# A first block normalized in two halves straight from PSUM, and a filter stage whose evacuations may run on either engine

## The chip, the cores and the metric

One core of a Trainium2 chip. The metric is the device time of one execution in microseconds, median of several; the profile's span is some 2 us shorter (129.6 us for a run of 131.36 us). PE is TensorE, DVE is VectorE, ACT is ScalarE, POOL is GpSimd. "Wait" means that an engine's next instruction is held by a semaphore. An execution counts as slow when it is over 1.5% above the fastest of its kernel; the others are the fast runs.

## The reference, cut to what matters

```python
x = A_x                                                       # (1, 2048, 512), bf16
h = x + irfft2(rfft2(layernorm(x)) * (w_r + 1j * w_i))         # the filter
h2 = h + mlp(layernorm(h))    # mlp: layernorm again, w1 over the sequence, gelu, w2 over the sequence
```

The kernel does the transforms as matmuls. The sequence is cut into 16 blocks n2 of 128 rows. After the filter each block must be transformed back (Bi, evacuation Bie, Ai), added to x, normalized (HH), and only then is it an operand of the first MLP product, which sums over the blocks (`m1_t_n2`, tile t of the hidden size). So the first block's way from the filter to HH is a serial chain.

## The kernel before

All instructions are placed by a builder: each has a name and one or several engines it may run on, and named lists fix the order per engine. The semaphores follow from the dependencies.

```python
    # filter stage: B (transform over d), evacuation Be, C (16 x 16 transform), evacuation Ce, product P with w, I, evacuation Ie
    NB = 4                                       # buffers of Bsb and of P
    K.op(f"Be{c}", "act", ...activation(Bb[c % NB], ps[:, b, :], ACT.Copy)...)         # ScalarE only
    K.op(f"Ce{tag}", "act", ...activation(dst, src, ACT.Copy)...)                      # ScalarE only
    ...
    # after the filter, blocks n2 = 0, 1, 2 ("early"): the identity matmul ID adds x inside PSUM
    def emit_h(n2):      # early blocks: copy PSUM to H
        K.op(f"h{n2}", "dve", ...tensor_copy(H[:, n2, :], ps[:, bA, :])...)
    def emit_sq(n2):     # sum of squares about the mean, ScalarE, from PSUM for early blocks
        K.op(f"sq{n2}", "act", ...activation(sq, hsrc, ACT.Square, bias=nm[:, n2, 0:1], accum_out=s2t[:, n2, 0:1])...)
    def emit_A2(n2):     # reciprocal root
        K.op(f"A2_{n2}", "act", ...activation(A2[:, n2, 0:1], s2t[:, n2, 0:1], ACT.Abs_reciprocal_sqrt, ...)...)
    def emit_hh(n2):     # normalize, from the copy in H
        K.op(f"hh{n2}", "dve", ...tensor_scalar(HH[:, n2, :], H[:, n2, :], nm[:, n2, 0:1], A2[:, n2, 0:1], op0=ALU.add, op1=ALU.mult)...)
    # later blocks: sd (sum and difference of the two parities) on VectorE, one Ai matmul, h = PSUM + x, sq, A2, hh
    ...
    "dve": "... P14 P15 Ie14_0 Ie15_0 Bie1 Bie2 h0 hh0 h1 sd3_1 sd3_0 hh1 h2"
```

In these lists a name is a group of instructions and its number the block or group: B, C, I, Bi, Ai are groups of matmuls on PE; a trailing e (Be, Ce, Ie, Bie) is the evacuation of such a group, its copy from PSUM to SBUF; P is a product with the filter weights on VectorE; m1 is the first MLP product; sd, sq, A2, h and hh are the steps of the normalization. HH is the normalized block that m1 reads.

## Time and profile before

| | before |
|---|---|
| time, median (range) | 131.52 us (131.19 to 131.54, 3 runs) |
| span of the profiled run | 129.6 us |
| busy: PE, DVE, ACT | 94%, 49%, 50% |
| filter, first to last matmul | 19.90 us |
| last filter matmul to first MLP matmul | 5.18 us |
| first MLP matmul to last matmul of all | 84.24 us |

The last three rows come from the starts of single matmuls in the trace. They are the measure used below, because the start of the filter itself moves between executions: in the 14 traces of this study it lay between 16.46 and 17.21 us, which is as large as most effects here. The sum of the three rows is 109.32 us. A start-to-start distance is the only fair look at PE: a shown matmul overlaps the next one (a 512-wide one is shown as 0.379 us and issued every 0.216), so PE looks busy where it idles by less than about 0.16 us. Some traces lack a few matmuls (nine in the one of before, none in the one of after, against the weight loads); a missing 512-wide one leaves a hole of exactly one issue time (0.216 us) and is not counted as idle.

### The profile page before, as it was taken

To read this page: it belongs to the slowest core of one execution; us is meant where nothing else is said; L and a number is where in the kernel's file an instruction comes from. 1 tells how busy PE (TensorE), PEld (TensorE's weight loads), DVE (VectorE), ACT (ScalarE), POOL (GpSimd) and SP (SyncE) were. 2 spreads that over 40 slices of the span, in tenths; PEclk is the share of its full clock that TensorE was granted. 3 is DMA by queue.
4 is the path that set the end of the run, shared out by engine and by line. 5 is a ranking of instruction groups with operands and counts; after the bars stand their busy time and mean duration, and the time that the engine had idled before them with its cause. 6 is when DMAs were issued, how large, how long until landed. Compare 5 with 4: busy or idle time off the path is not lost.

```text
span 129.6 us, 2028 instructions
## 1 busy us (share of the span) xinstructions
PE 122.1 (94%) x772; PEld 73.5 (57%) x781; DVE 63.5 (49%) x135; ACT 64.3 (50%) x137; POOL 11.8 (9%) x33
## 2 busy tenths in 40 slices
PE   6969989999998999999999999999999999999990
PEld 2346667777764455555444444456666666666660
DVE  1699917999948767668664000000422423323322
ACT  4699879989968487787787932222000000000000
POOL 0068980200000000000000000000000000000000
DMA  3999888999999999999000000000112112121121
GB/s 83 369 395 366 239 216 182 281 337 378 403 419 411 427 416 420 273 331 374 33 0 0 0 0 0 5 0 0 40 40 81 40 55 69 42 77 44 40 81 43
DMA packets 16505, 22.71 MB, mean 175 GB/s; under 512 B 1552, under 2 KB 12304, under 8 KB 16368
## 3 DMA queue, kind: packets, MB, share of 16 engines
q1 hardware_dynamic: 15808, 21.66, 48.2%
q10 hardware_dynamic: 576, 0.92, 1.9%
q0 software_dynamic: 112, 0.01, 0.3%
q8 instruction: 6, 0.10, 0.3%
q14 instruction: 3, 0.02, 0.0%
HBM read 20.49 MB, written 2.10 MB: 174 GB/s over the span
## 4 chain that ended last, share of the span: by engine, by line
PE 82%; DMA 5%; ACT 3%; SPq 3%; DVE 2%; issue 1%; POOL 0%; DVEq 0%; ACTq 0%
PE ps L839 29%; PE ps L919 27%; DMA F<-c_F 5%; PE ps L769 5%; PE ps L690 5%; PE ps L637 5%; PE ps L651 3%; SPq L490 3%; PE ps L806 2%; PE ps L593 2%; PE ps L925 2%; ACT Xsb L664 2%; ACT Y L607 1%; ACT Bsb L641 1%; DVE OUT L931 1%
## 5 line engine op out<-in xcount | busy, mean ns | idle before, releaser
L839 PE MATMUL ps<-HH,W 128*128 128x512 bf16 (+1 forms) x172 | 41.4, 379 | 0.7 <-DVE HH L831 0.6
L919 PE MATMUL ps<-GT,W 128*128 128x512 bf16 (+1 forms) x162 | 35.7, 379 | 0.2
L931 DVE SCALAR_TENSOR_TENSOR OUT<-ps,B2f,H 128x512 bf16<-128x512 f32 x16 | 12.0, 752 | 44.8 <-PE ps L919 24.4
L919 PEld LDWEIGHTS ps<-GT,W 128*128 128x128 bf16 (+1 forms) x165 | 23.8, 144 | 11.9
L839 PEld LDWEIGHTS ps<-HH,W 128*128 128x128 bf16 (+1 forms) x176 | 16.8, 100 | 18.4 <-issue 1.3
L901 ACT ACTIVATE GT<-ps,B1f 128x512 bf16<-128x512 f32 (+1 forms) x11 | 7.0, 692 | 10.8 <-PE ps L839 10.8
L815 DVE TENSOR_TENSOR H<-ps,X 128x512 bf16<-128x512 f32 x13 | 9.0, 691 | 6.8 <-PE ps L806 6.8
L672 DVE TENSOR_TENSOR P<-Xsb,W 128x1024 bf16<-128x1024 bf16 x16 | 10.5, 686 | 3.6 <-ACT Xsb L664 3.6
L821 ACT ACTIVATE SQ<-H,nm 128x512 bf16<-128x512 bf16 x13 | 9.4, 721 | 4.7 <-DVE H L815 4.7
L559 DVE BATCH_NORM_STATS2 st<-X 128x6 f32<-128x512 bf16 x13 | 8.2, 677 | 3.2 <-DMA X<-in_A_x_dram 3.2
L769 PE MATMUL ps<-GD,TT 128*128 128x256 bf16 x64 | 9.6, 273 | 0.1
L779 ACT ACTIVATE EO<-ps 128x512 bf16<-128x512 f32 x14 | 8.1, 581 | 2.6 <-PE ps L769 2.6
L690 PE MATMUL ps<-Hm,P 128*128 128x128 bf16 x128 | 9.3, 220 | 0.1
L641 ACT ACTIVATE Bsb<-ps 128x512 bf16<-128x512 f32 x16 | 8.8, 613 | 0.7 <-PE ps L637 0.7
L593 PE MATMUL ps<-FS,X 128*128 128x256 bf16 x64 | 7.8, 272 | 1.3 <-POOL FS L577 1.3
L637 PE MATMUL ps<-E,Y 128*128 128x256 bf16 x64 | 8.3, 273 | 0.7 <-ACT Y L607 0.7
L664 ACT ACTIVATE Xsb<-ps 128x1024 bf16<-128x1024 f32 (+1 forms) x10 | 8.6, 873 | 0.7 <-PE ps L651 0.4
L690 PEld LDWEIGHTS ps<-Hm,P 128*128 128x128 bf16 x128 | 7.5, 98 | 2.0 <-issue 1.3
L769 PEld LDWEIGHTS ps<-GD,TT 128*128 128x128 bf16 x64 | 6.1, 97 | 3.9 <-ACT TT L706 0.4
L577 POOL TENSOR_SCALAR FS<-F,rs 128x256 bf16<-128x256 bf16 x16 | 7.4, 482 | 7.6 <-ACT rs L565 7.2
L533 PE MATMUL ps<-WM 128*128 128x512 bf16 (+1 forms) x19 | 6.6, 500 | 1.2 <-DVE eps L525 1.2
L593 PEld LDWEIGHTS ps<-FS,X 128*128 128x128 bf16 x64 | 5.5, 97 | 3.7 <-POOL FS L577 2.3
(51 smaller groups left out, 92.7 us busy)
## 6 DMA issues: line engine op xcount, KB each, us to landing
W<-in_B_w_dram SPq DMA_DIRECT2D x8, 688.0 KB, 12.2
W<-in_B_w_dram SPq DMA_DIRECT2D x10, 512.0 KB, 18.0
out_dram<-OUT SPq DMA_DIRECT2D x16, 128.0 KB, 1.7
X<-in_A_x_dram SPq DMA_DIRECT2D x4, 256.0 KB, 6.1
F<-c_F SPq DMA_DIRECT2D x4, 256.0 KB, 6.4
IF<-c_IF SPq DMA_DIRECT2D x1, 1024.0 KB, 7.8
W<-in_A_w_r_dram SPq DMA_DIRECT2D x4, 224.0 KB, 3.6
W<-in_A_w_i_dram SPq DMA_DIRECT2D x4, 224.0 KB, 3.7
```

The lines of the kernel that those rows point to most:

```text
L593: r = eng.matmul(ps[:, b, 256 * u:256 * u + 256].rearrange("p (a b) -> p a b", a=2), X[:, n2, 128 * t:128 * t + 128], fr if t < 2 else fa, ...
L637: r = eng.matmul(o, Y[:, k, c, :], E[:, k, :].rearrange("p (h r) -> p h r", h=2), start=(i == 0), stop=(i == 3), skip_group_check=True)
L641: K.op(f"Be{c}", "act", lambda e, eng: eng.activation(Bb[c % NB][:, :], ps[:, b, :], ACT.Copy), ins=[ps[:, b, :]], outs=[Bb[c % NB][:, :]] ...
L664: K.op(f"Ce{tag}", "act", lambda e, eng: eng.activation(dst, src, ACT.Copy), ins=[ps[:, b, :] for b in banks], outs=[Xb[i][:, :, cs[0] % 2 ...
L672: return eng.tensor_tensor(P[:, :, :, :], x.unsqueeze(2).broadcast_to([NP, 2, 2, 256]), W[:, 2 * c:2 * c + 2, :, :], ALU.mult)
L690: r = eng.matmul(o, P[:, h, m, par::2], Hm[:, v, m, :].rearrange("p (m r) -> p m r", r=4), start=(h == 0 and m == 0 and (par == 0 or b != ...
L769: r = eng.matmul(o, TT[:, q, n2, par, :], GD[:, par, q, :], start=(i == 0), stop=(i == 3), skip_group_check=True)
L815: K.op(f"h{n2}", "dve", lambda e, eng: eng.tensor_tensor(H[:, n2, :], ps[:, bA, :], X[:, n2, :], ALU.add), ins=[ps[:, bA, :], X[:, n2, :]] ...
L821: K.op(f"sq{n2}", "act", lambda e, eng: eng.activation(sq[:, :], hsrc, ACT.Square, bias=nm[:, n2, 0:1], accum_out=s2t[:, n2, 0:1]), ins=[h ...
L839: return eng.matmul(ps[0:Mt, bank, :], W1[:, n2, 128 * t:128 * t + Mt], HH[:, n2, :], start=(n2 == 0), stop=(n2 == 15), skip_group_check=True)
L919: r = eng.matmul(ps[:, b, :], W2[t][0:Kt, n2::16], GT[0:Kt, t, :], start=(t == 0), stop=(t == NFT - 1), skip_group_check=True)
L931: K.op(f"fin{n2}", "dve", lambda e, eng, n2=n2, b=b: eng.scalar_tensor_tensor(OUT[:, n2, :], ps[:, b, :], B2f[:, n2:n2 + 1], H[:, n2, :], ...
```

## The change

The intent: (a) take the first block past the filter in two halves of d, in banks of their own, with statistics by `bn_stats` on VectorE and the normalization straight from PSUM, the copy to H later; (b) a newly searched order for the first twelve blocks; blocks 1 and 2 also normalized from PSUM; (c) in the filter, B and C evacuations on either engine, six buffers of Bsb and P, and a new order. Its core:

```diff
-    NB = 4
+    NB = 6
-        K.op(f"Be{c}", "act", ... activation ...)
+        K.op(f"Be{c}", ("act", "dve"), ... activation if e == "act" else tensor_copy ...)
-        K.op(f"Ce{tag}", "act", ... activation ...)
+        K.op(f"Ce{tag}", ("act", "dve"), ... activation if e == "act" else tensor_copy ...)
 # PSUM banks of the early blocks moved: bank_E 1:3 2:4 3:2, else 7; bank_A 1:5 2:0, else 6
     def emit_hh(n2):
+        src = ps[:, bank_A(n2), :] if n2 < NEARLY else H[:, n2, :]
-        ... tensor_scalar(HH[:, n2, :], H[:, n2, :], nm, A2 ...)
+        ... tensor_scalar(HH[:, n2, :], src, nm, A2 ...)
+    def emit_first():                      # block 0; m = 0, 1: left half in bank 6, right half in bank 7
+        ID0m, Bi0m (two matmuls each), Bie0m (256 wide, either engine), Ai0em, Ai0om
+        bq0m: bn_stats(sc[:, 6*m:6*m+6], ps[:, bk, 0:256])      # VectorE
+        aq0:  bn_aggr(sc[:, 16:18], sc[:, 0:12])
+        A2_0: activation(A2[:, 0, 0:1], sc[:, 17:18], Abs_reciprocal_sqrt, ...)
+        hh0m: tensor_scalar(HH[:, 0, half m], ps[:, bk, 0:256], nm, A2)
+        h0m:  copy of the half to H, prio 63                     # after the normalization
+    for t in range(NACC): for m in range(2): m1_t_0{l,r}         # first MLP matmuls of block 0 in halves
 # per-engine lists, filter part:
-  pe  "B0 B1 B2 B3 C0 C1 B5 B4 C2p I0 B7 B6 I1 C4p I3 B8 B9 C6p I2 B10 B11 I4 C8p I5 ... I9 B15 I8 C14 I10 C15 I11 I12 I13 I14 I15"
+  pe  "B0 B1 B2 C0 B3 C1 B5 B4 C2p I0 B6 B7 C4p B8 B9 I1 C6p I2 B10 I3 B11 C8p ... B15 I7 I8 I9 C14 C15 I10 I11 I12 I13 I14 I15"
-  dve "... P0 P1 Ie0 P3 P2 Ie1 Ie3 P4 P5 ... Bie1 Bie2 h0 hh0 h1 sd3_1 sd3_0 hh1 h2"
+  dve "... Be2 P0 Be5 P1 Ie0 Be6 P2 P3 Be8 P5 P4 ... P15 Ie13 Ie15_0 Bie00 bq01 bq00 aq0 hh01 hh00 h01 h00 sd3_1 sd3_0 hh1 h3 sd4_1 sd4_0 h1 hh2 ..."
```

## The prediction

> **What bounds the kernel now.** I read the page first: busy shares, then the chain that ended last.
>
> ```profile
> span 129.6 us, 2028 instructions
> PE 122.1 (94%) x772; PEld 73.5 (57%) x781; DVE 63.5 (49%) x135; ACT 64.3 (50%) x137; POOL 11.8 (9%) x33
> PE 82%; DMA 5%; ACT 3%; SPq 3%; DVE 2%; issue 1%; POOL 0%; DVEq 0%; ACTq 0%
> ```
>
> PE (TensorE) carries 82% of the chain; no other engine exceeds 5%. But a shown matmul overlaps its neighbours, so a busy share hides small gaps. I therefore cut the span where the stages meet, and compare each stretch with the issue time of its matmuls (columns: stretch, its length, then each engine's busy time and count).
>
> ```profile
> 16.79:36.96 20.17, 19.98 (x257) 15.56 (x259) 16.25 (x26) 18.44 (x32) 3.21 (x8) 1.00 0.99 312
> 36.96:41.87 4.91, 4.30 (x30) 2.54 (x29) 2.97 (x7) 3.33 (x10) 0.00 (x0) 1.00 1.01 414
> 41.87:68.06 26.19, 26.03 (x141) 13.04 (x145) 18.75 (x53) 20.13 (x52) 0.00 (x0) 1.00 0.77 285
> 68.06:88.47 20.41, 20.31 (x95) 9.63 (x95) 1.42 (x3) 8.74 (x15) 0.00 (x0) 1.00 0.00 1
> 88.47:126.53 38.06, 37.86 (x172) 25.06 (x174) 11.28 (x16) 0.67 (x1) 0.00 (x0) 1.00 0.15 52
> ```
>
> These are the filter (16.79 to 36.96), the way from the filter to the first MLP matmul, the inverse transform interleaved with the first MLP product, the rest of that product, and the second product. The last holds 176 matmuls: 38.06/176 = 0.216 us each, full rate. The third holds about 84 MLP matmuls and 13 inverse ones of 512 columns (97 x 0.216 = 20.95) and 12 blocks of four 256-column ones (0.435 each in the chain, 5.2): 26.15 of 26.19, no gap. So from 41.87 on the end is fixed by PE work; only what PE idles before can be won, and what it would idle newly is lost.
>
> In the filter, chain pieces give 0.87 for two B groups, 0.45 for an I group after a B and 0.55 after a C, 0.54 for a pair of Cs, 0.33 for a single C. 16 B (6.96), 7 C pairs (3.78), 2 singles (0.66), 16 I (7.12) and some 9 changes after a C at 0.1 (0.9) are 19.4 of 20.17: about 0.75 us idle. Between 36.96 and 41.87 PE has two warm-up matmuls, three identity, three A groups of two 512-equivalents and four B groups: 5 x 0.216 + 3 x 0.43 + 4 x 0.435 = 4.1 of 4.91, so 0.8 idle. That idle time is mostly one wait:
>
> ```profile
> 40.99 0.27 PE L802 MATMUL ps<-EO,IF 128*128 128x256 bf16 x1
> 41.87 1.24 PE L839 MATMUL ps<-HH,W 128*128 128x512 bf16 x5 [0.61 <-DVE HH L831]
> ...
> 39.91 0.69 DVE L780 CAST EO<-ps 128x512 bf16<-128x512 f32 x1 [0.40 <-PE ps L769]
> 40.51 0.68 DVE L812 CAST H<-ps 128x512 bf16<-128x512 f32 x1
> 41.31 0.41 DVE L831 TENSOR_SCALAR HH<-H,nm,A 128x512 bf16<-128x512 bf16 x1
> ```
>
> VectorE evacuates block 2, copies block 0 to H and normalizes from the copy; only then has PE its first MLP operand.
>
> **What the Trainium skill says.** "TensorE: Matmul & The Clock Gate", Back-to-back issue gap, gives 518 cycles for 512 columns and 262 for 256, or 216 and 109 ns at 2.4 GHz. The trace agrees (0.216; 0.435 for four of 256), so halving a matmul costs almost no streaming. "Perfetto Trace Analysis", Optimizing Scalar/DVE Operations, says that breaking up instructions may let work complete sooner where ScalarE or VectorE makes bubbles, at a fixed cost per access: a 512-wide VectorE copy from PSUM takes 0.692 us here, a 256-wide one 0.415, not half. "VectorE: DVE Perf Modes", Why PSUM operands drop a tier, holds that an fp32 PSUM operand runs at the slow rate: normalizing from bf16 SBUF takes 0.41 here, a 512-wide PSUM read 0.69. So two halves from PSUM will take about 0.77 together against 0.41, in exchange for not waiting for the copy.
>
> **The change, part by part.**
>
> (a) First block. I start from the filter's end at 36.96 as before and walk the new order. Bi00 begins at 37.55 (before: 37.53), ends 37.94; its 256-wide VectorE evacuation (0.415) ends 38.4. Bi01 ends 38.16, ScalarE's 256-wide copy (0.384) 38.6. The four half A matmuls issue from 38.46 to 38.9; the first finished half is readable at 38.95. Two half bn_stats: estimate 0.41 each (512-wide: 0.68, less the 0.27 by which the two copy widths differ), 0.35 apart, to 39.76; aggregate 0.17, to 39.97; reciprocal root 0.29 on ScalarE after block 1's evacuation, to 40.35; two half normalizations 0.41 each, 0.34 apart, to 41.1. First MLP matmul at about 41.2, against 41.87. PE meanwhile does the same other work (to about 41.1). Gain: 0.67.
>
> (b) Interleaved stage. The first block's six MLP matmuls become twelve halves: 12 x 0.109 = 6 x 0.216, nothing. But VectorE has more to do early: two half copies to H and normalizations of blocks 1 and 2 from PSUM at 0.69 instead of 0.41; block 2's copy goes to ScalarE. Walking the fixed order, PE waits about 0.1 for block 3's sum/difference, 0.1 for a bank behind block 4's evacuation, 0.05 for block 2's normalization, 0.1 for another evacuation, all before 47. Later VectorE owes 0.69+0.41+0.49 = 1.59 per block while PE takes 1.95 as before, so it catches up. Loss: about 0.45, where before had none.
>
> (c) Filter. The matmuls and the number of C groups are the same, so PE's 19.4 stays. Before, ScalarE does all 16 B and all 10 C evacuations and 6 of the 17 inverse ones; at spacings of 0.49, 0.92 (double C), 0.55 (single C) and 0.49 this is 18.3 us of the 19.9 between its first and last. After, 7 B, one single C go to VectorE and 11.5 inverse evacuations to ScalarE: 16 - 7 = 9 x 0.49, 6 x 0.92, 3 x 0.55, 11 x 0.49 + 0.3 = 17.2. VectorE goes from 16 x 0.60 + 10 x 0.61 + 0.34 = 16.0 to 16 x 0.60 + (7+1+4) x 0.61 + 0.34 = 17.3, starting at 18.3 rather than 20.0. So both are level, each near 17.3 of 19.4, and six buffers let B run ahead and I lag. The last product must be ready about 35.8; VectorE's load up to it is 16.3, from 18.3 to 34.7, plus its waits: about 1 us of slack. I expect 0.3 of the 0.75 to come back. C0 and C1 are split by a B but C14 and C15 joined, which cancels.
>
> (d) Memory. Two more Bsb and P buffers move an overlaid second-product weight tile, which is not needed before 88. No effect.
>
> Sum: 0.67 - 0.45 + 0.3 = 0.5, rounded up to 0.6 because an order found by search was presumably kept for some gain. 131.52 - 0.6 = 130.9.
>
> **Rivals.**
>
> VectorE becomes the filter's bound. It then alternates evacuations and products in a strict order, and each product stands behind an evacuation that waits for PE. For it: 17.3 of 19.4 us, and now two engines instead of one feed every step. Against: the added lag of the I groups. If each of the eight double steps slipped 0.1, the filter would lose 0.5: about 131.7 in all.
>
> The first block's gain is given back in full, because the strict order puts later PE work behind VectorE. For it: the stretch from 41.87 had no gap at all, and VectorE is full from 40.5 to 43.6. The time would be 131.2 with the filter's gain, 131.5 without.
>
> Both idle times close: 0.75 + 0.8 = 1.55, or 130.0. This is the floor: nothing here shortens PE's work, so a gain over 2% (128.9) would need what this change doesn't touch.
>
> A transfer becomes the bound. The first MLP weights were issued at 28.06 and landed after 9.0 us, at 37.1; the second filter-weight piece lands about 23.75 and I need it about 24.3. Close, but earlier than either use; a slip would be worth some 0.3.
>
> **Range and chances.** Estimates from 130.0 (both idle times gone) to 131.7 (filter slips, first block gives back) span the cases; I take 130.1 to 131.7. Faster by over 2%: 0.03. Within 2%: 0.95. Slower by over 2% (134.1): 0.02.
>
> **What would show it.** The first MLP matmul should start some 4.2 us after the filter's last matmul instead of 4.9. The stretch after it, to the point where the MLP matmuls run alone, should be longer than 26.2 by 0.3 to 0.6, with PE waiting for HH, SD or EO. The filter should take 19.7 to 20.0, with ScalarE less busy by 1 us and VectorE more. From there on the two products must be unchanged at 0.216 per matmul. I am wrong if the filter moves by over 0.6 either way, if PE waits over 1 us after the first MLP matmul, or if a weight's landing appears among the waits.

## More of the kernel before

The groups of the kernel before that the argument needs, kept apart by shape (columns: busy us, mean ns of one, idle before):

```profile
L831 DVE TENSOR_SCALAR HH<-H,nm,A 128x512 bf16<-128x512 bf16 x16 | 6.5, 406 | 1.0 <-ACT A L826 0.9
L812 DVE CAST H<-ps 128x512 bf16<-128x512 f32 x3 | 2.0, 683 | 0.0
```

The normalization is cheap (406 ns) only because it reads a bf16 copy in SBUF, and the copy costs 683 ns ahead of it.

## The result, and the profile after

The changed kernel takes 130.73 us (130.59 to 130.84, 4 runs) against 131.43 us (131.19 to 131.54, 4 runs). The ratio is 0.9949 with a 95% interval of 0.9931 to 0.9967. Ratios here are the mean time of one kernel's fast runs over that of the other's of the same rounds, so not quite the ratio of the medians. 130.73 lies 0.17 us below the predicted 130.9.

The page of the kernel after, its span, busy shares and the chain that ended last:

```profile
span 128.9 us, 2052 instructions
PE 121.7 (94%) x789; PEld 74.6 (58%) x789; DVE 65.5 (51%) x140; ACT 63.8 (49%) x136; POOL 12.5 (10%) x33
PE 88%; ACT 4%; DMA 3%; DVE 1%; POOL 1%; issue 1%
```

Still PE, and more of the chain than before: 88% against 82%.

The stretches of the kernel after, cut at the same events as before (stretch, length, busy time and count per engine):

```profile
16.79:36.91 20.12, 20.12 (x257) 15.48 (x258) 17.47 (x29) 17.90 (x30) 3.85 (x8) 1.00 0.99 302
36.91:41.38 4.47, 4.20 (x32) 2.74 (x31) 2.96 (x8) 3.29 (x8) 0.00 (x0) 1.00 1.02 419
41.38:65.76 24.38, 24.38 (x142) 13.44 (x143) 19.47 (x54) 20.02 (x55) 0.00 (x0) 1.00 0.87 322
65.76:87.61 21.85, 21.85 (x103) 10.34 (x101) 1.42 (x3) 8.72 (x14) 0.00 (x0) 1.00 0.00 1
87.61:125.89 38.28, 38.24 (x177) 25.22 (x175) 11.26 (x16) 0.69 (x1) 0.00 (x0) 1.00 0.15 52
```

The first stretch, the filter, is as long as before (20.12 against 20.17), although VectorE took over more than 1 us of work (17.47 against 16.25) and ScalarE lost 0.5. The second is 0.44 shorter. The border between the third and the fourth lies elsewhere in the new order, so they are read together: 46.23 us here, against 46.60 there, of which about 0.2 is where the last window begins (before, the first matmul of the second product is missing from the trace). In starts of matmuls:

| us | filter | last filter mm to first MLP mm | first MLP mm to last mm | sum |
|---|---|---|---|---|
| before | 19.90 | 5.18 | 84.24 | 109.32 |
| after | 19.85 | 4.74 | 84.09 | 108.68 |
| difference | -0.05 | -0.44 | -0.15 | -0.64 |

The sum accounts for the 0.7 us of the time and of the span. It is idle time of PE that went: from start to start PE idled 0.41 us in the filter, 0.99 on the way and 0.37 after it before the change, and 0.36, 0.55 and 0.18 after it. The two products run at the same pace as before.

The way to the first MLP matmul in the kernel after, in order of time (start, length, engine), on PE:

```profile
40.84 0.27 PE L804 MATMUL ps<-EO,IF 128*128 128x256 bf16 x1
41.38 0.49 PE L910 MATMUL ps<-HH,W 128*128 128x256 bf16 x3 [0.27 <-DVE HH L885]
```

and on VectorE:

```profile
38.87 0.76 DVE L879 BATCH_NORM_STATS2 sd<-ps 128x6 f32<-128x256 f32 x2 [0.67 <-PE ps L876]
39.66 0.21 DVE L881 BATCH_NORM_AGGREGATE sd<-sd 128x2 f32<-128x12 f32 x1
40.24 1.00 DVE L885 TENSOR_SCALAR HH<-ps,nm,A 128x256 bf16<-128x256 f32 x2 [0.36 <-ACT A L882]
41.15 0.75 DVE L891 CAST H<-ps 128x256 bf16<-128x256 f32 x2
```

The copy (now L891) comes after the normalization and off the path. But two halves of the normalization take 1.00 us, and PE still idles 0.43 us (40.84 + 0.11 to 41.38). Groups by shape:

```profile
L836 DVE TENSOR_SCALAR HH<-ps,nm,A 128x512 bf16<-128x512 f32 x2 | 1.6, 804 | 0.0
L885 DVE TENSOR_SCALAR HH<-ps,nm,A 128x256 bf16<-128x256 f32 x2 | 1.0, 540 | 0.4 <-ACT A L882 0.4
L891 DVE CAST H<-ps 128x256 bf16<-128x256 f32 x2 | 0.7, 416 | 0.0
```

A normalization from PSUM is 120 ns dearer than a copy of the same width (804 against 683, 540 against 416). The prediction had set it equal to the copy.

In the MLP stretch the kernel before did have small holes, which the prediction missed: in its timeline, four 256-wide matmuls starting at 49.00 should hand over at 49.44, but the next starts at 49.50.

```profile
49.00 0.60 PE L769 MATMUL ps<-GD,TT 128*128 128x256 bf16 x4
49.50 0.59 PE L839 MATMUL ps<-HH,W 128*128 128x512 bf16 x2
```

The next HH ends at 49.35. Such a hole of 0.06 us recurs in every second block; with one late one there are six of them, 0.37 us. HH is no later in these blocks than in those between: the following one ends at 51.36, and its matmul starts on time at 51.44. What differs is that a new piece of the MLP weights is due (they are loaded two blocks at a time): in the packed trace each of the six has, ahead of its weight load, an instruction of 0.051 us on PE that only waits for a semaphore, and the blocks without a hole have none. After the change HH is mostly ready well before PE reads it (the one that ends at 49.40 is read at 49.81), and there are two holes, 0.086 and 0.090 us.

### The profile page after: what moved, and what is told of

Read it like the earlier page. It is cut to its first block, busy times and chain, and to the rows that moved or that the text cites. A ratio compares the mean times of both kernels' runs of the same rounds, so it can differ in the third digit from the quotient of the medians.

```text
span 128.9 us, 2052 instructions
## 1 busy us (share of the span) xinstructions
PE 121.7 (94%) x789; PEld 74.6 (58%) x789; DVE 65.5 (51%) x140; ACT 63.8 (49%) x136; POOL 12.5 (10%) x33
## 4 chain that ended last, share of the span: by engine, by line
PE 88%; ACT 4%; DMA 3%; DVE 1%; POOL 1%; issue 1%
PE ps L844 29%; PE ps L962 28%; PE ps L692 6%; PE ps L637 6%; PE ps L593 5%; PE ps L771 5%; PE ps L652 3%; DMA X<-in_A_x_dram 3%; PE ps L808 2%; PE ps L968 2%; ACT Y L607 1%; PE ps L910 1%; ACT SQ L552 1%; ACT SQ L555 1%; DVE HH L885 1%; POOL FS L577 1%
## 5 line engine op out<-in xcount | busy, mean ns | idle before, releaser
L844 PE MATMUL ps<-HH,W 128*128 128x512 bf16 (+1 forms) x170 | 39.9, 379 | 0.0
L781 ACT ACTIVATE EO<-ps 128x512 bf16<-128x512 f32 x15 | 8.9, 592 | 3.6 <-PE ps L771 3.3
L637 PE MATMUL ps<-E,Y 128*128 128x256 bf16 x64 | 8.8, 274 | 0.7 <-ACT Y L607 0.7
L771 PE MATMUL ps<-GD,TT 128*128 128x256 bf16 x60 | 9.0, 273 | 0.0
L665 ACT ACTIVATE Xsb<-ps 128x1024 bf16<-128x1024 f32 (+1 forms) x9 | 8.0, 883 | 0.5 <-PE ps L652 0.4
L637 PEld LDWEIGHTS ps<-E,Y 128*128 128x128 bf16 x64 | 5.6, 98 | 2.5 <-issue 1.1
```

The source lines that it names most:

```text
L637: r = eng.matmul(o, Y[:, k, c, :], E[:, k, :].rearrange("p (h r) -> p h r", h=2), start=(i == 0), stop=(i == 3), skip_group_check=True)
L771: r = eng.matmul(o, TT[:, q, n2, par, :], GD[:, par, q, :], start=(i == 0), stop=(i == 3), skip_group_check=True)
L781: return eng.activation(eo[:, :], ps[:, bE, :], ACT.Copy)
L844: return eng.matmul(ps[0:Mt, bank, :], W1[:, n2, 128 * t:128 * t + Mt], HH[:, n2, :], start=(n2 == 0), stop=(n2 == 15), skip_group_check=True)
```

## The experiments

The effects are a few tenths of a microsecond, so the trace decides (lengths as in the table above), and times and ratios only confirm.

### The two halves of the change alone

e1 takes only the filter's part of the change, e2 only the rest:

```diff
 e1: kernel before
+  NB = 6, six Bsb and P buffers, Be and Ce on either engine, filter part of the lists from the changed kernel
 e2: changed kernel
+  NB = 4, four buffers, Be and Ce on ScalarE, filter part of the lists from the kernel before
```

> The kernel before with only the changed filter stage (six buffers, evacuations on either engine, new order); first block and MLP stage as before. My theory, from the two traces: PE bounds the filter in both kernels, so it ends only about 0.05 us earlier; the first MLP matmul starts about 0.05 us earlier than the 41.87 us of before, total -0.05 us, ratio 0.999 to 1.001. Rival, the term of my prediction: the filter gives 0.3 us, ratio about 0.998, and the first MLP matmul at 41.6 us or before.

Measured: 131.14 us against 131.34, ratio 0.9975 (0.9944 to 1.0006). Filter 19.85, then 5.16, then 84.24: the sum is 0.07 us under that of before. The first MLP matmul started at 41.73, but the filter had started 0.07 earlier than in the trace of before. The wide interval can't tell the two expectations apart; the trace can: the filter gives 0.05 us.

> The changed kernel with the filter stage of before; only the first block and the MLP order are changed. My theory: nearly the whole gain of 0.7 us stays (0.6 to 0.7), ratio 0.995; the distance from the filter's last matmul to the first MLP matmul is about 0.5 us shorter than in the kernel before. Rival: the two parts need each other (the searched order starts from another state of the engines), and the gain falls to 0.4 us or less, ratio 0.997 or above.

Measured: 130.84 us, ratio 0.9952 (0.9918 to 0.9985). Filter 19.91, then 4.73, then 84.09: the sum is 0.59 us under before. The parts add up (0.07 + 0.59 = 0.66 against 0.64 for both), so they do not need each other. The six small holes before the MLP matmuls are there in e1 and gone in e2, so it is not the filter but parts (a) and (b), which e2 holds together, that removed them.

### The normalization from PSUM without halves

```diff
 e3: kernel before
-  dve "... Bie1 Bie2 h0 hh0 h1 ..."          hh0 reads H
+  dve "... Bie1 Bie2 hh0 h0 h1 ..."          hh0 reads PSUM, whole (512 wide)
```

> The kernel before with one step changed: block 0 is normalized straight from PSUM, whole, ahead of its copy to H, no halves, no new statistics. Theory: the 0.61 us of the copy leaves the path, the normalization takes 0.80 us instead of 0.41, and the first MLP matmul starts about 0.25 us earlier (41.6 us); ratio about 0.998. If the halves are what matters, the gain is under 0.1 us and the first MLP matmul stays at 41.8 us or later.

Measured: 132.14 us (median of six, one of them slow; 131.78 for the five fast ones), ratio 1.0045 (0.9997 to 1.0094) where the theory had 0.998. The way to the first MLP matmul fell from 5.18 to 4.88, as the theory said, but the MLP stretch grew from 84.24 to 84.80. PE in e3, in order of time:

```profile
41.71 1.24 PE L840 MATMUL ps<-HH,W 128*128 128x512 bf16 x5 [0.30 <-DVE HH L832]
43.34 0.39 PE L806 MATMUL ps<-SD,IF 128*128 128x512 bf16 x1 [0.39 <-DVE SD L791]
```

The five MLP matmuls are issued by 42.78, and block 3's Ai waits until 43.34 for its sum and difference, which stand on VectorE behind the copies of blocks 0 and 1. The work taken from the path is still VectorE's, and comes back one wait later: 0.30 won, 0.56 lost. Reading PSUM directly gives two thirds of the first-block gain (0.30 of 0.44). To keep it, the order after it would have to change too; no run tests that alone, but the changed kernel puts block 1's copy behind the sum and difference, block 1's normalization and blocks 3's and 4's work.

### The halves in the order in which they are finished

In the changed kernel VectorE finishes the right half first, but PE wants the left half first and idles 0.43 us. e4 turns that round:

```diff
 e4: changed kernel
-  start=(m == 0) ... pe "... Ai2 m1_3_0l m1_4_0l m1_4_0r Bi4 m1_2_0l m1_1_0l Ai3 m1_2_0r m1_1_0r m1_3_0r Bi5 ..."
+  start=(m == 1) ... pe "... Ai2 m1_3_0r m1_4_0r m1_2_0r m1_1_0r m1_3_0l m1_4_0l m1_2_0l Bi4 m1_1_0l Ai3 Bi5 ..."
 e6: as e4, and the right half's copy on ScalarE ahead of block 1's square, Bi4 earlier
+  act "... Bie3 h01 sq1 ..."   pe "... m1_3_0r m1_4_0r m1_2_0r Bi4 m1_1_0r m1_3_0l ..."
```

> The changed kernel with the first MLP halves in the order in which VectorE finishes them: right halves of four tiles first, then the left ones, with the accumulation start flag on the right half. In the changed kernel PE idles 0.43 us for the left half while the right one is done. Theory: PE starts the right halves about 40.95 us instead of 41.38 and the total falls by 0.3 to 0.45 us against the changed kernel, to 130.3 us, ratio to before 0.991 to 0.992. Rival: the idle time only moves to the next wait (the fourth block's bank, the sum and difference of block 3), and the total stays within 0.1 us of 130.7.

Measured: 130.52 us, ratio 0.9927 (0.9894 to 0.996). The first MLP matmul came 0.44 us sooner (4.30 instead of 4.74), and the MLP stretch was 0.43 us longer (84.52). Sum 108.67, against 108.68: no gain, and the slightly lower median is within what the start of the filter alone moves. The theory fell; the rival had named the place, the fourth block's bank (the time is 0.08 us under the range it gave):

```profile
40.87 0.93 PE L910 MATMUL ps<-HH,W 128*128 128x256 bf16 x7
41.63 0.60 PE L771 MATMUL ps<-GD,TT 128*128 128x256 bf16 x4
...
42.27 0.39 PE L808 MATMUL ps<-SD,IF 128*128 128x512 bf16 x1
42.92 0.50 PE L771 MATMUL ps<-GD,TT 128*128 128x256 bf16 x3 [0.26 <-ACT EO L781]
```

PE has used up the halves that filled later holes, and stands from 42.48 to 42.92 until block 4's evacuation frees the bank.

> The right-halves-first order, with the right half of block 0 copied to H by ScalarE ahead of block 1's square, so that the fourth block's bank comes free 0.4 us earlier and its B group may stand after three right halves. In the right-halves-first run the 0.44 us won before the first MLP matmul came back as a wait of 0.44 us for the fourth block's evacuation. Theory: that wait falls to 0.1 to 0.3 us, and the first MLP matmul to the end of the MLP falls by 0.15 to 0.3 us; total about 130.3 to 130.5 us, ratio to before 0.990 to 0.993. Rival: the later square delays block 1's normalization, and the wait moves there; total 130.6 to 130.8 us.

Measured: 130.68 us, ratio 0.9939 (0.9915 to 0.9964); 4.30, then 84.54; sum 108.70. The wait for block 4's evacuation did fall, to 0.26 us, but one of 0.31 us for block 2's normalization took its place at 44.64. Again no gain, and a time in the rival's range, but not for its reason: block 1's normalization is no later. In the changed kernel, e4 and e6 alike the HH of blocks 1 and 2 end 6.37 to 6.39 and 8.69 to 8.71 us after the filter's last matmul, whatever PE does before.

e13 asks what the later waits are made of, by leaving out block 0's copies to H. Its result is wrong on purpose (relative error 0.35).

```diff
 e13: e6 without h00 and h01; the last addition of block 0 reads H[:, 1, :]
```

> Wrong on purpose in block 0 (the last addition reads block 1's rows). The right-halves-first kernel with block 0's copies to H left out, which takes 0.75 us of work from VectorE and ScalarE between 40.6 and 41.5 us. In the kernels with the early right halves, what the first MLP matmul gained (0.44 us) came back in the MLP stretch (84.52 to 84.55 us against 84.09). If it is VectorE's and ScalarE's work on the first blocks that takes it back, the MLP stretch falls to 84.1 to 84.3 us at an unchanged 4.30 us before it. If it is the chain of block 1's own statistics (square, root, normalization), it stays at 84.45 or more.

Measured: 130.63 us, ratio 0.9937 (0.9897 to 0.9976); 4.30, then 84.28, sum 108.43. So 0.26 us of the 0.44 come back when 0.75 us of evacuation work is gone. This is inside the range of the first theory. The HH of blocks 1 and 2 now end at 6.02 and 8.44, 0.36 and 0.25 us sooner. What is left (84.28 against 84.09) is one hole of 0.27 us before block 2's MLP matmuls, the same wait as in e6. From about 41 to 45 us PE is fed no faster than VectorE and ScalarE prepare blocks 1 to 4, and an earlier first matmul only moves its idle time.

### What the filter hangs on

> The changed kernel with the freedom taken away in the filter: B and C evacuations all on ScalarE, the inverse ones shared as in the kernel before; six buffers and PE's new order stay. If PE bounds the filter, its last matmul stays within 0.15 us of the changed kernel's. If the evacuations bound it as soon as they are not level (ScalarE near 18.3 us of the 19.9), it comes 0.3 to 1 us later and the total is 131 to 131.7 us.

```diff
 e9: changed kernel, B and C evacuations all in ScalarE's list, in the order of PE's groups; inverse evacuations shared as before; VectorE's products in a matching order
```

Measured: 132.56 us, ratio 1.0085 (1.0059 to 1.0111). The filter took 21.69 us, 1.84 more; the rest was unchanged (4.73, 84.09). Longest waits of VectorE's products and PE's C groups in e9 (who waits, for whom, total, times, longest):

```profile
DVE P L674 <- ACT Xsb L665: 5.1, 4, 2.7
...
PEld ps L652 <- ACT Xsb L665: 1.2, 4, 0.6
...
PEld ps L652 <- ACT Bsb L641: 0.8, 3, 0.4
```

> The changed kernel with four Bsb and P buffers instead of six, order and engines unchanged. PE's new order runs B groups up to four ahead of their C and products up to six ahead of their I group, so with four buffers the writers must wait for the readers: if the new order lives on the buffers, the filter grows by 0.5 us or more; if PE alone counts, it stays within 0.15 us of 19.85.

```diff
 e12: changed kernel
-    NB = 6
+    NB = 4
```

Measured: 132.04 us, ratio 1.0036 (0.9997 to 1.0075). Filter 20.96 us, 1.11 more. The wait is one of 0.93 us in PE's C14/C15 at 33.65, behind this on VectorE:

```profile
32.74 1.30 DVE L674 TENSOR_TENSOR P<-Xsb,W 128x1024 bf16<-128x1024 bf16 x2 [1.13 <-PE ps L692]
33.95 0.69 DVE L642 CAST Bsb<-ps 128x512 bf16<-128x512 f32 x1
```

A product waits 1.13 us for PE to release its buffer, and Be15 behind it is late for C15. So with PE's new order it costs 1.84 us to take the freedom away (in the one pair of lists that was tried) and 1.11 us to take the buffers, and yet all three together are worth 0.05 us against the old order with neither: each seems to make up for what the others ask.

Then: is it PE? In both kernels PE's filter holds 18 passages into or out of a stretch of C matmuls, which use half of the array's rows; each costs 0.092 to 0.096 us between the starts, 1.7 us together. Beyond these PE idles 0.41 us in the filter before and 0.36 after, the latter all ahead of the last three I groups, which wait for VectorE's last three products. Three runs tried to take something from that:

```diff
 e5:  pe  "B0 B1 B2 B3 C0 C1 ..."  instead of  "B0 B1 B2 C0 B3 C1 ..."          (16 passages instead of 18)
 e10: dve "... P8 P9 Ie5 P11 ..."  instead of  "... P8 Ie5 P9 P11 ..."          (VectorE idles 0.24 us before Ie5)
 e11: both
```

> The changed kernel with C0 and C1 side by side again (B3, C0, C1 instead of C0, B3, C1), so one stretch of half-height matmuls less; each way into and out of such a stretch costs PE 0.09 us in the traces. If PE bounds the filter throughout, its last matmul comes 0.19 us earlier (about 36.45 instead of 36.64) and the total falls by as much. Rival: the end of the filter waits for VectorE's products (two gaps of 0.16 us before the last I groups in the changed kernel), C0 is 0.43 us later, the products with it, and the filter ends no earlier or up to 0.4 us later.

Measured: 130.54 us, ratio 0.9935 (0.9908 to 0.9963). Filter 19.83, sum 108.66. The two passages (0.19 us) are gone, but PE waits 0.05 us at C2/C3 for an evacuation (0.15 with the passage that is there anyway) and 0.18 instead of 0.05 before I13; the filter is 0.03 us shorter. This trace does not decide between the expectations, though. C14 came 0.16 us sooner after the filter's start than in the changed kernel, as the theory has it, but VectorE was late for it:

```profile
30.10 0.69 DVE L709 CAST TT<-ps 128x512 bf16<-128x512 f32 x1 [0.24 <-PE ps L692]
30.93 1.90 DVE L674 TENSOR_TENSOR P<-Xsb,W 128x1024 bf16<-128x1024 bf16 x3
```

Product 9 starts 0.84 us after the evacuation ahead of it, not 0.61: it waited for the last piece of the filter weights, which landed at 30.91 in this execution (29.68 in that of the changed kernel), and from there VectorE runs to product 15 without a pause. With the weights in time the filter would have been some 0.15 us shorter; that is an estimate from these starts, and no trace shows it. The median is 0.19 us under e8's of the same rounds, with intervals that overlap.

> The changed kernel with two neighbours on VectorE swapped: product 9 ahead of the evacuation of inverse group 5, which makes VectorE idle 0.24 us in the changed kernel. If VectorE's products set the end of the filter (the two gaps of 0.16 us and one of 0.05 before the last three I groups), the filter shrinks from 19.85 to 19.6 to 19.7 us. If it is PE, it stays at 19.85. Third possibility: product 9 then waits for the last piece of filter weights, which landed at 29.7 to 30.9 us in these runs where product 9 would start at 29.6: then the gain is lost in proportion, and the filter stays at 19.8 or more.

Measured: 130.87 us, ratio 0.9958 (0.9917 to 0.9999). Filter 19.85, unchanged. VectorE is earlier up to product 12, and then waits for PE at the evacuation of C14:

```profile
32.77 0.68 DVE L674 TENSOR_TENSOR P<-Xsb,W 128x1024 bf16<-128x1024 bf16 x1
33.69 0.69 DVE L665 CAST Xsb<-ps 128x512 bf16<-128x512 f32 x1 [0.24 <-PE ps L652]
34.30 1.89 DVE L674 TENSOR_TENSOR P<-Xsb,W 128x1024 bf16<-128x1024 bf16 x3
```

> The swap of product 9 together with C0 and C1 side by side. Merging alone left the filter at 19.83 us, as 0.19 us fewer changes were taken back by waits of 0.15 and 0.14. If VectorE's lateness took them, the swap returns 0.1 to 0.2 us and the filter takes 19.5 to 19.7; if the early wait of 0.15 and the weights take them, it stays at 19.75 to 19.85.

Measured: 130.78 us, ratio 0.9946 (0.9909 to 0.9983). Filter 19.75, sum 108.57: together they give 0.10 us where each alone gave 0.03 or nothing. Here the timeline shows the wait for the filter weights (0.41 us ahead of product 9), and from it on VectorE again runs to product 15 without a pause:

```profile
29.75 0.69 DVE L674 TENSOR_TENSOR P<-Xsb,W 128x1024 bf16<-128x1024 bf16 x1 [0.41 <-DMA W<-in_A_w_i_dram]
```

So the filter has limits in series. Up to C14/C15 it is PE, with hardly a hole; after them VectorE must do one evacuation and the last three products at 0.60 us each, while PE's I groups take 0.445. Moving VectorE's work forward does nothing as long as it then waits for C14 (e10). Close behind lie the weights: their last piece landed 12.4 to 13.8 us after the filter's start in the 14 traces, and product 9 of the changed kernel started 13.7 us after it, 0.83 us later than its own landing. Both runs that relieve PE, e5 and e11, ran into them; what the merge is worth with the weights in time is not shown.

A last control, the changed kernel again:

> The changed kernel as it is, for the same chip: 130.7 us, ratio to before 0.995, first MLP matmul 4.74 us after the filter's last one.

Measured: 130.73 us, ratio 0.9949 (0.9924 to 0.9973); 19.85, 4.73, 84.09. The lengths repeat to 0.01 us. No run beats the changed kernel clearly: e11 is 0.11 us shorter in the trace and 0.05 us longer by the medians, and e4 and e5, 0.2 us shorter by the medians, are level in the trace.

## Why the prediction was right

The time was right, the range held it, and the sum of the terms (0.52, called 0.6) is close to the measured 0.64 to 0.70. That it is so close is luck: (b) was too low by 0.60 us, (a) and (c) together too high by 0.48.

- **What bounds it** (PE from 41.87 on, only idle time to win): right. What changed is PE idle time. "No gap" in the stretch from 41.87 was wrong by 0.3 to 0.4 us: I took 84 matmuls from the count of weight loads, where 83 were issued (80 recorded and three missing), and so explained the holes away.
- **(a) First block, predicted gain 0.67, measured 0.44.** The mechanism is right; the mis-sized term is "two half normalizations 0.41 each, 0.34 apart". They took 0.54 each, 1.00 together instead of 0.75, because a tensor_scalar with two per-partition operands from PSUM costs 0.12 us more than a copy of its width. The other steps of the walk fit: half bn_stats 0.42, evacuations 0.42 and 0.38, start of the normalization 40.24 against 40.35.
- **(b) Interleaved stage, predicted loss 0.45, measured gain 0.15.** This step failed: the walk gave PE new waits and took away none. Of the four small waits (0.35 us as listed, not 0.45), two came (0.086 and 0.090 us), and the six of 0.06 that the old order had, which I had not seen, were gone. e1 and e2 show that this is not the filter's doing. The idea behind it, that VectorE's early work is given back later, is sound: e3 lost 0.56 us that way, e4 and e6 all of their 0.44. What avoided it here is argued only: the new order postpones block 1's copy and gives block 2's to ScalarE, and no run undoes these alone.
- **(c) Filter, predicted gain 0.3, measured 0.05.** The step that failed is VectorE's "about 1 us of slack" before the last product. Its load was as walked, but its waits from 18.31 on came to 1.4 us (what its starts lie apart beyond 0.60), so the last product ended at 36.11, and PE stood 0.36 us ahead of the last three I groups. There was also less to win: of the 0.75 us that I called idle only 0.41 was. 0.22 of the rest is a warm-up matmul that the trace lacks: the window ended at 36.96, but two weight loads for warm-up matmuls stand ahead of it, and one matmul of 0.216 us fits in between:

```profile
36.69 0.15 PEld L533 LDWEIGHTS ps<-WM 128*128 128x128 bf16 x2
36.96 0.38 PE L533 MATMUL ps<-WM 128*128 128x512 bf16 x1
```

(The next window was charged with both, so 0.99 us was idle there and not 0.8.) The other 0.12 is PE's work, 19.54 us and not 19.4. The 18 passages were in that sum, for 0.54 for a pair of Cs and 0.33 for a single one hold one each. That both engines end up level is right, and so is that neither the weights nor the two added buffers cost anything in the changed kernel's trace.

- **Rivals.** "VectorE becomes the filter's bound" is half true, for the last three products only, and it took the gain of (c). "The gain is given back in full" did not happen to the change, but did to three of its variants. "A transfer becomes the bound" was not so, but near: in e5 and e11 it is there.
- **Signs.** Of those named beforehand the two products at 0.216 held. The first MLP matmul came 4.47 us after the filter by the same windows (said: 4.2), the stretch after it was shorter and not 0.3 to 0.6 longer, the filter's window was 20.12 (said: 19.7 to 20.0), ScalarE lost 0.5 us (said: 1). None of the three signs of being wrong showed in the changed kernel.

What stays open: whether the evacuation of C14 behind product 13 would recover part of the filter's last 0.36 us; e10's wait of 0.24 suggests it, and it was not run. Also what e5's merge is worth when the weights land in time. Also why the start of the filter moves by up to 0.75 us between executions; it lies before the filter, in a stage that no run touched.

## What to carry to other kernels

When an engine is full but has small holes, measure them from start to start, compare the matmuls with the weight loads, and only then call the rest idle: here 0.22 of the presumed 0.75 us was a matmul that the trace lacked. Taking work off the path does not take it off the engine; ask which instruction will now stand behind it, and change the order there at the same time. And judge changes of a few tenths of a microsecond by lengths within the trace, not by total times, when the start of the filter alone moves more than that. Look in each such trace for a transfer that happened to land late before calling a variant useless, as in e5.

## What the Trainium skill lacked or had wrong

- "TensorEngine Tiling (Array Packing)", Key Properties, says that changing the tiling mode drains TensorE, without a figure. Here each change, in as well as out, cost 0.092 to 0.096 us between full-height matmuls and those on 64 rows; 18 of them were 1.7 us of a 19.9 us filter.
- "TensorE: Matmul & The Clock Gate", Back-to-back issue gap, gives 131 ns per matmul for 512 columns and 81 for 128 in a stream with weight loads, and calls the 216 and 56 ns of its formula isolated figures. In these traces, with a weight load for each matmul, it was 216 ns for 512 columns and 55.6 for 128, as the formula has it.
- "VectorE: DVE Perf Modes", the perf-mode tier table, puts tensor_copy and tensor_scalar in one row. From PSUM at the same width a tensor_scalar with two per-partition scalars took 0.12 us longer (804 against 683 ns for 512 elements, 540 against 416 for 256). No page that I read has this.
